# Two attention-mixer layers on one core: later blocks' queries projected inside attention, with a second guard

## The chip, the core and the metric

One of the eight cores of a Trainium2 chip runs the whole kernel. The time is the device's, from start to end of one execution, in microseconds (us). The engines that matter are PE (TensorE, matmuls), ScalarE (ACT in the rows: exponentials, casts), VectorE (DVE), GpSimd (POOL) and SP (SyncE), whose queue issues nearly all DMAs.

## The reference, cut to what matters

```python
def _A_ref(x, wq, wk, wv, wo):            # x: (1, 2048, 512), 32 heads of 16
    q = (x @ wq).reshape(B, S, H, Dh).transpose(0, 2, 1, 3)
    k = x @ wk                            # one key head and one value head for all
    v = x @ wv
    scores = einsum("bhqd,bkd->bhqk", q, k) * Dh ** -0.5
    o = einsum("bhqk,bkd->bhqd", softmax(scores), v)
    return o.transpose(0, 2, 1, 3).reshape(B, S, H * Dh) @ wo

def _B_ref(x, w1, b1, w2, b2):            # MLP over the tokens, F = 1792
    u = gelu(einsum("bsd,sf->bdf", layernorm(x), w1) + b1)
    return (einsum("bdf,fs->bds", u, w2) + b2).transpose(0, 2, 1)

for layer in range(2):
    x = x + _A_ref(layernorm(x), wq, wk, wv, wo)
    x = x + _B_ref(layernorm(x), w1, b1, w2, b2)
```

## The kernel before, in words

The residual x stays in SBUF as 16 tiles of 128 tokens. Four tiles make a block of 512 (NB = 4). Every layer has three parts: a projection, attention, and the MLP over the tokens, and each overlaps its neighbours where the order of the code lets it. That order is written out by hand: the order of calls is the order on every engine, and each engine takes its own instructions in it.

**Projection (class Proj).** A fp32 product is made of three products of parts: an operand is cast to a short form (hi) and the rest of it is a second tile (lo). `weights` does this for wq and wk, wv (L190 to L200; the lo parts on VectorE). For a block, `norm` and `turn` make the transposed normalized rows; `keys` (L274) gives keys and values, `key_terms` (L285) puts the keys' hi and lo parts with six DMAs (L293) into `kst`, the score's left operand; `queries(b, m)` (L315) multiplies a quarter of the query columns, which are 12 matmuls of 512 columns (L265), takes their squares on ScalarE (L323), splits them into hi (ScalarE, L271) and lo (VectorE, L272) in a tile `q2`, and puts that tile into a DRAM buffer `qd` with two DMAs of 256 KB on SP (L336), here called a pair of puts. Four quarters make a block, so sixteen products and sixteen pairs make the queries of a layer. `q2` and the key tile `ks` come from one ring of buffers with the tag "q2": three in layer 0, two in layer 1. A new tile waits until the DMAs of the one whose buffer it takes have landed.

**The shift and the guard.** Softmax is computed without a maximum: a bound made of the norms of queries (`bound`, L341: four small matmuls with `sel`) and of keys (`key_bound`, L357) is put into one extra row of both score operands and so subtracted inside the score. In before, the keys' part is written into row 0 of `kst` (L371) and copied by a DMA into row 64 (L372). Where the bound is too far off, true maxima are needed: `flag` works out whether, and `guard` (L408) reads the flag on every engine (L410) and branches (L414). For these inputs the branch is not taken. So that the wait is covered, before scores ten tiles ahead of the guard (`Attention.ahead`, L621) and splits a query product in two around other work (`within`, L266).

**Attention (class Attention).** A group is four heads of one block of queries; 8 groups to a block, 32 in a layer. `load_group` (L471) brings a group's operands from `qd` into one of two tiles `qs` by four DMAs. A group has 32 tiles of scores, each of 2x512 columns: two matmuls (L581), one exponential of 128x1024 on ScalarE (L588), two matmuls that sum into one PSUM bank (L594); VectorE evicts the bank at a group's end (L504). `run` (L652) interleaves tiles and other PE work in turns: LONG holds 12 tiles and one fill, SHORT 8 tiles and a fill, PLAIN 2 tiles without. Fills of the class Mixer are products of w1 (L795, from group 8 on) and output projections (L570, from group 4 on).

**MLP.** After attention, `second` (L965) multiplies with w2, bound by PE. Layer 1's projection is woven into layer 0's `second` stage for blocks 0 to 2, and the rest of it comes as a tail behind that stage.

```python
LONG = (3, 0, 3, -4, 2, -2, 2, -2, 2, -4)
SHORT = (2, 0, 2, -4, 2, -2, 2, -2)
PLAIN = (2, -2)
```

A positive number scores so many tiles, a negative one sums so many, 0 is the fill.

Of the kernel before, what the change touches and what calls it, by code (L numbers as in the profile page):

```python
# [8 lines left out]
F32 = mybir.dt.float32  # L9
# [9 lines left out]
P = 128  # L19
S, D, H, DH, F = 2048, 512, 32, 16, 1792  # L20
NB = 4
# [16 lines left out]
AHEAD = 2  # L38
# [7 lines left out]
def kernel(  # L46
# [43 lines left out]
    k2m = cp.tile([1, NB], F32, tag="k2m", name="k2m")  # L90
    qd = dp.tile([NB * NG, R1, 4, 2, QB], F32, tag="qd", name="qd")
# [9 lines left out]
    def constants():  # L101
# [15 lines left out]
        for i in range(NQ):  # L117
            for r in (0, HALF):
                nc.gpsimd.memset(f32(qs[i][r : r + 1]), 1.0)
# [15 lines left out]
    def stats(ts_, name):  # L135
        n = len(ts_)
        st = sm.tile([P, 4, 6], F32, tag="st", name=f"st_{name}")
        mv = sm.tile([P, 4, 2], F32, tag="mv", name=f"mv_{name}")
        for i, t in enumerate(ts_):
            nc.vector.bn_stats(st[:, i, :], x[t])  # L140
        for i, t in enumerate(ts_):
            nc.vector.bn_aggr(mv[:, i, :], st[:, i, :])
        return mv[:, :n, :]

    def rstd(mv, twice, name):
        n = mv.shape[1]
        w = sm.tile([P, 4, 4], F32, tag="rw", name=f"rw_{name}")
# [26 lines left out]
    class Proj:  # L174
        def __init__(self, layer):
            self.l = layer
            self.sides = 0
            self.sq, self.h, self.hT, self.kv, self.kk = {}, {}, {}, {}, {}
            self.pool = pool(f"proj{layer}")
            p = self.pool  # L180
            self.wq = p.tile([P, ND, 2, D], F32R, tag="wq", name=f"wq{layer}")
            self.wkv = p.tile([P, ND, 2, 2 * DH], F32R, tag="wkv", name=f"wkv{layer}")
            self.c2 = p.tile([H, 2, QB], F32R, tag="c2", name=f"c2_{layer}")

        def weights(self):
            p, n = self.pool, self.l
            nc.gpsimd.memset(f32(self.c2), 0.0)
            for kt in range(ND):
                raw = p.tile([P, D], F32, tag="tmp", bufs=7 - 3 * n, name=f"wqr{n}_{kt}")
                nc.sync.dma_start(raw, wq_d[kt * P : (kt + 1) * P, :])  # L190
                nc.scalar.copy(self.wq[:, kt, 0, :], raw)
                nc.vector.tensor_tensor(
                    self.wq[:, kt, 1, :], raw, f32(self.wq[:, kt, 0, :]), op=ALU.subtract
                )
            raw = p.tile([P, ND, 2 * DH], F32, tag="kvr", name=f"wkvr{n}")
            nc.sync.dma_start(raw[:, :, :DH], wk_d.rearrange("(t p) c -> p t c", p=P))
            nc.sync.dma_start(raw[:, :, DH:], wv_d.rearrange("(t p) c -> p t c", p=P))
            nc.vector.tensor_copy(self.wkv[:, :, 0, :], raw)
            nc.vector.tensor_tensor(
                self.wkv[:, :, 1, :], raw, f32(self.wkv[:, :, 0, :]), op=ALU.subtract  # L200
            )

        def stats(self, ts_):
            self.mv = stats(ts_, f"a{self.l}_{ts_[0]}")

        def scales(self, ts_):
            n, mv, k = self.l, self.mv, len(ts_)
            y = rstd(mv, False, f"a{n}_{ts_[0]}")
            my = sm.tile([P, 4], F32, tag="my", name=f"my{n}_{ts_[0]}")
# [3 lines left out]
            self.y = y, my  # L213

        def norm(self, ts_, scalar=True):
            p, n = self.pool, self.l
            y, my = self.y
            for i, t in enumerate(ts_):
                self.h[t] = p.tile([P, D], F32, tag="tmp", bufs=7 - 3 * n, name=f"h{n}_{t}")
# [4 lines left out]
                else:  # L224
                    normed(self.h[t], t, self.mv, y, i)

        def turn(self, ts_):

            p, n, k = self.pool, self.l, len(ts_)
            b, c = ts_[0] // 4, ts_[0] % 4 * P  # L230
            if c == 0 and b not in self.hT:
                self.hT[b] = p.tile([P, ND, 2, QB], F32R, tag="hT", bufs=2 - n, name=f"hT{n}_{b}")
# [26 lines left out]
        def product(self, out, w, cols, b, within=None):  # L259
            k, hT = 0, self.hT[b]  # L260
            for kt in range(ND):
# [5 lines left out]
                if within and kt == 1:  # L267
                    within()

# [862 lines left out]
```

## Time and profile before

| what | us |
|---|---|
| median of 3 runs | 2712.18 |
| lowest and highest run | 2710.46, 2713.71 |
| the profiled execution | 2709.55 |
| its span (first to last instruction) | 2707.8 |
| PE busy | 2637.9 (97%) |
| ScalarE busy | 2126.4 (79%) |
| exponentials (2048 of 128x1024) | 1907.1, 1.057 each |
| VectorE busy | 818.4 (30%) |
| GpSimd busy | 87.3 (3%) |

The profile is of one execution; its rows give a start time, a length, the engine, the line (L), the operation with the names of output and input, shapes and a count, and in brackets how long the engine stood idle just before and what released it. SPq is the queue of SP. A busy PE is not the same as PE at its peak: when the exponentials set the pace, its matmuls are stretched.

### The profile page before, as it was taken

To read this page: it belongs to the slowest core of one execution; us is meant where nothing else is said; L and a number is where in the kernel's file an instruction comes from. 1 tells how busy PE (TensorE), PEld (TensorE's weight loads), DVE (VectorE), ACT (ScalarE), POOL (GpSimd) and SP (SyncE) were. 2 spreads that over 40 slices of the span, in tenths; PEclk is the share of its full clock that TensorE was granted. 3 is DMA by queue.
4 is the path that set the end of the run, shared out by engine and by line. 5 is a ranking of instruction groups with operands and counts; after the bars stand their busy time and mean duration, and the time that the engine had idled before them with its cause. 6 is when DMAs were issued, how large, how long until landed. Compare 5 with 4: busy or idle time off the path is not lost. (4 is left out here: it accounts for less than half of the span.)

```text
span 2707.8 us, 40615 instructions
## 1 busy us (share of the span) xinstructions
PE 2637.9 (97%) x16062; PEld 1225.8 (45%) x16062; DVE 818.4 (30%) x1835; ACT 2126.4 (79%) x2399; POOL 87.3 (3%) x124
## 2 busy tenths in 40 slices
PE   7699999999999999999998999999999999999999
PEld 4323333433444343368774333344434333434787
DVE  6312123223322332155443111322242224222532
ACT  3389999899898999953325999998898999997511
POOL 1000000000000000040000000000000000001300
PEclk9899999999999999999999999999999999999999
DMA  3210011111111011023332101011111111110343
GB/s 129 94 49 21 23 35 38 45 30 34 38 38 35 26 42 31 11 78 113 107 102 73 30 21 35 23 44 30 41 28 39 38 41 32 38 25 14 110 123 99
DMA packets 159553, 135.51 MB, mean 50 GB/s; under 512 B 12862, under 2 KB 127612, under 8 KB 159356
## 3 DMA queue, kind: packets, MB, share of 16 engines
q1 hardware_dynamic: 159356, 132.85, 16.9%
q8 instruction: 128, 2.10, 0.3%
q14 instruction: 69, 0.57, 0.1%
HBM read 93.47 MB, written 22.02 MB: 43 GB/s over the span
## 5 line engine op out<-in xcount | busy, mean ns | idle before, releaser
L588 ACT ACTIVATE p<-sc 128x1024 f32<-128x1024 f32 x2048 | 1907.1, 1057 | 161.4 <-PE sc L581 161.4
L594 PE MATMUL acc<-p,vaug 128*32 128x512 f32 x8192 | 1124.0, 603 | 0.3 <-DVE q L272 0.3
L581 PE MATMUL sc<-qs,kst 51*128 51x512 f32 x4096 | 737.5, 442 | 28.2 <-DMA kst<-kst 8.9
L581 PEld LDWEIGHTS sc<-qs,kst 51*128 51x128 f32 x4096 | 318.8, 185 | 777.9 <-issue 514.5
L594 PEld LDWEIGHTS acc<-p,vaug 128*32 128x32 f32 x8192 | 233.0, 108 | 442.4 <-issue 412.3
L965 PE MATMUL py<-u,w 128*128 128x512 f32 x1344 | 307.7, 390 | 0.0
L965 PEld LDWEIGHTS py<-u,w 128*128 128x128 f32 x1344 | 251.8, 188 | 53.1 <-issue 0.7
L795 PE MATMUL pu<-hb,w 128*128 128x512 f32 x984 | 248.4, 401 | 0.4 <-POOL w L782 0.4
L795 PEld LDWEIGHTS pu<-hb,w 128*128 128x128 f32 x984 | 178.4, 188 | 59.8 <-issue 15.2
L953 ACT CAST w<-w2r 128x896 fp32r<-128x896 f32 x64 | 60.0, 944 | 181.7 <-PE py L965 164.0
L504 DVE COPY ev<-acc 128x512 f32<-128x512 f32 x64 | 44.3, 692 | 518.8 <-PE acc L594 518.4
L524 DVE RECIPROCAL o<-o 128x128 f32<-128x128 f32 x120 | 113.6, 947 | 99.8 <-DMA o<-ev 99.8
L573 DVE TENSOR_TENSOR x<-x,po 128x512 f32<-128x512 f32 x64 | 44.0, 688 | 311.5 <-PE po L570 311.5
L803 DVE TENSOR_TENSOR ua<-ua,pu 128x512 f32<-128x512 f32 x54 | 36.9, 687 | 324.6 <-PE pu L795 324.6
L782 POOL TENSOR_TENSOR w<-w1r,w 128x256 fp32r<-128x256 f32 x74 | 59.1, 816 | 2214.7 <-ACT w L780 2214.7
L265 PE MATMUL pq<-hT,wq 128*128 128x512 f32 x384 | 101.5, 417 | 0.1
L570 PE MATMUL po<-wo,hl 128*128 128x512 f32 x360 | 100.4, 412 | 0.9 <-DVE ev L504 0.6
L954 DVE TENSOR_TENSOR w<-w2r,w 128x896 fp32r<-128x896 f32 x64 | 69.8, 1091 | 101.7 <-ACT w L953 101.0
L795 PE MATMUL pu_l<-hb,w 128*128 128x512 f32 x336 | 80.1, 394 | 4.9 <-POOL hb L895 3.4
L265 PEld LDWEIGHTS pq<-hT,wq 128*128 128x128 f32 x384 | 75.0, 200 | 21.0 <-issue 3.0
L801 DVE COPY ua<-pu 128x512 f32<-128x512 f32 x28 | 19.4, 692 | 199.0 <-PE pu L795 199.0
L570 PEld LDWEIGHTS po<-wo,hl 128*128 128x128 f32 x360 | 62.6, 188 | 35.0 <-issue 19.3
(129 smaller groups left out, 913.2 us busy)
## 6 DMA issues: line engine op xcount, KB each, us to landing
w1r<-in_B_w_dram SPq DMA_DIRECT2D x224, 128.0 KB
w2r<-in_B_w_dram SPq DMA_DIRECT2D x64, 448.0 KB
qs<-qd SPq DMA_DIRECT2D x128, 136.0 KB
qd<-q SPq DMA_DIRECT2D x64, 256.0 KB
o<-ev SPq DMA_DIRECT2D x120, 128.0 KB
qs<-qd SPq DMA_DIRECT2D x128, 64.0 KB
x<-in_A_x_dram SPq DMA_DIRECT2D x16, 256.0 KB
out_dram<-x SPq DMA_DIRECT2D x16, 256.0 KB
```

What stands on the lines that cost most here:

```text
L265: nc.tensor.matmul(out, a, c, start=(k == 0), stop=(k == 3 * ND - 1))
L504: nc.vector.tensor_copy(ev, acc)
L524: nc.vector.reciprocal(o[:, 1, c], o[:, 1, c])
L570: nc.tensor.matmul(po, a, c, start=(k == 0), stop=(k == 3 * len(parts) - 1))
L581: nc.tensor.matmul(sc[:, j, :], kst[rows, kt * P : (kt + 1) * P], qs[i % NQ][rows, j0 // 2, :], start=True, stop=True,)
L588: nc.scalar.activation(pt, sc, AF.Exp, scale=0.25)
L594: nc.tensor.matmul(self.acc[i][c : c + 32, :], vaug[:, kt].rearrange("p d k -> p (d k)"), pt[:, j, :], start=(kt == 0), stop=(kt == NKT - ...
L782: eng.tensor_tensor(w[:, 1], raw, f32(w[:, 0]), op=ALU.subtract)
L795: nc.tensor.matmul(pu, a, c, start=(start and k == 0), stop=(stop and k == 5))
L953: nc.scalar.copy(w[:, 0], raw)
L954: nc.vector.tensor_tensor(w[:, 1], raw, f32(w[:, 0]), op=ALU.subtract)
L965: nc.tensor.matmul(py, a, d, start=(c == 0 and f == 0 and k == 0), stop=(c == 1 and f == NFH - 1 and k == 2),)
```

## The change

Constant NOW = (1, 3) says how many blocks of queries are projected before attention begins: one in layer 0, three in layer 1. The other blocks' products, shifts and the minimum over their bounds come as fills of attention's first turns (`later`): in layer 0 twelve LONG and four SHORT turns, 176 tiles from the start of group 0 on; in layer 1 four LONG and two SHORT. A fill writes the spare one of the two accumulator banks; both its parts hi and lo are made on VectorE, its squares on GpSimd. A second guard for the later blocks stands between the tiles where those blocks begin, after 8 groups in layer 0 and after 24 in layer 1. The Mixer's pools open when the last of these fills is done.

The keys' part of the bound leaves the score: rows 0 and 64 of `kst` and `qs` become zero, and a small matmul with a row of ones (`onerow`) spreads a quarter of the keys' bound to 128 partitions (`kb`), which each exponential adds as its bias. No tile is scored ahead of the guard, no product is split, and no put is held back until after it.

In layer 0 the weights are issued on ScalarE's queue, so the loads of x follow one another on SP; the lo parts of weights and of keys go from VectorE to GpSimd, and GpSimd's constants now stand behind the weights' lo parts. The statistics of blocks 2 and 3 are taken together. The ring of `q2` and `ks` has two buffers in both layers, and in layer 0 keys and queries take turns in it. In layer 1, products (2, 0) and (2, 1) move from the stage of w2 into the tail behind it, and block 3's four products into attention.

```diff
-AHEAD = 2
+NOW = (1, 3)
...
         nc.gpsimd.memset(f32(kst), 1.0)
-        for i in range(NQ):
-            for r in (0, HALF):
-                nc.gpsimd.memset(f32(qs[i][r : r + 1]), 1.0)
+        nc.gpsimd.memset(onerow, 1.0)
+        for r in (0, HALF):
+            nc.gpsimd.memset(f32(kst[r : r + 1]), 0.0)
+            for i in range(NQ):
+                nc.gpsimd.memset(f32(qs[i][r : r + 1]), 0.0)
...
         def weights(self):
             p, n = self.pool, self.l
+            issue = nc.sync if n else nc.scalar
...
+            nc.scalar.copy(self.wkv[:, :, 0, :], raw)
+            nc.gpsimd.tensor_tensor(
                 self.wkv[:, :, 1, :], raw, f32(self.wkv[:, :, 0, :]), op=ALU.subtract
             )
+            for kt in range(ND):
+                nc.scalar.copy(self.wq[:, kt, 0, :], raws[kt])
+                nc.gpsimd.tensor_tensor(
+                    self.wq[:, kt, 1, :], raws[kt], f32(self.wq[:, kt, 0, :]), op=ALU.subtract
+                )
...
-            ks = p.tile([DH, 2, QB], F32R, tag="q2", bufs=3 - n, name=f"ks{n}_{b}")
-            self.split(ks, kv[:DH, :])
+            ks = self.keep.tile([DH, 2, QB], F32R, tag="q2", bufs=2, name=f"ks{n}_{b}")
+            nc.scalar.copy(ks[:, 0, :], kv[:DH, :])
+            nc.gpsimd.tensor_tensor(ks[:, 1, :], kv[:DH, :], f32(ks[:, 0, :]), op=ALU.subtract)
...
+        def queries(self, b, m, pq=None):
+            k, n = self.keep, self.l
+            during = pq is not None
+            if not during:
+                pq = bank2(f"pq{n}_{b}_{m}")[:, 0, :]
+            self.product(pq, self.wq, slice(m * P, (m + 1) * P), b)
+            q2 = k.tile([P, 2, QB], F32R, tag="q2", bufs=2, name=f"q2_{n}_{b}_{m}")
+            sq = self.sq[b, m] = k.tile([P, QB], BF16, tag="sq", bufs=5, name=f"sq{n}_{b}_{m}")
+            (nc.vector.tensor_copy if during else nc.scalar.copy)(q2[:, 0, :], pq)
+            nc.vector.tensor_tensor(q2[:, 1, :], pq, f32(q2[:, 0, :]), op=ALU.subtract)
+            if during:
+                nc.gpsimd.tensor_tensor(sq, f32(q2[:, 0, :]), f32(q2[:, 0, :]), op=ALU.mult)
             else:
+                nc.scalar.activation(sq, pq, AF.Square)
...
         def key_bound(self):
...
-            self.key_shift(k2)
-            self.k2 = k2
+            pb = self.side(f"pkb{n}")
+            nc.tensor.matmul(pb[:, :1], onerow, k2, start=True, stop=True)
+            nc.vector.tensor_scalar(kb, pb[:, :1], 0.25, None, op0=ALU.mult)
...
+        def later(self):
+            n, now = self.l, NOW[self.l]
+            work = []
+            for b in range(now, NB):
+                for m in range(ND):
+                    work.append((LONG, lambda i, b=b, m=m: self.queries(b, m, bank(i, f"pq{n}_{b}_{m}"))))
+                work.append((SHORT, lambda i, b=b: self.shifts(b, bank(i, f"pc{n}_{b}"))))
+            work.append((SHORT, lambda i: self.lowest(now, NB, bank(i, f"pg{n}_{now}"))))
+            return work
...
-            nc.scalar.activation(pt, sc, AF.Exp, scale=0.25)
+            nc.scalar.activation(pt, sc, AF.Exp, bias=kb, scale=0.25)
...
+            second_guard = 2 * NKT * NG * NOW[self.l]
+            later = proj.later()
             while self.scored < total:
                 mix.chores(self)
-                turn = mix.turn() if len(self.pend) == LAG else PLAIN
+                turn, part = PLAIN, None
+                if len(self.pend) == LAG:
+                    if later:
+                        turn, part = later[0]
+                    else:
+                        turn, part = mix.turn(), lambda i: mix.fill(self, i)
...
+                if self.scored == second_guard:
+                    proj.guard(proj.flagged, NOW[self.l], NB)
...
+    proj.shifts(0)
+    proj.key_bound()
+    proj.lowest(0, NOW[0])
+    proj.first_groups()
+    proj.first_guard()
...
             proj.scales(tiles(b)[3:])
             proj.norm(tiles(b)[3:], False)
+            proj.queries(b - 1, 0)
+            proj.turn(tiles(b)[:2])
+            proj.queries(b - 1, 1)
+            proj.turn(tiles(b)[2:])
             proj.queries(b - 1, 2)
-            proj.turn(tiles(b)[:2])
+            proj.keys(b)
             proj.queries(b - 1, 3)
-            proj.turn(tiles(b)[2:])
-            proj.keys(b)
-            proj.last_keys()
```

Where instructions stand, first on SP in layer 0's projection, behind the loads of x. In a name such as q_0_1_0 the figures are layer, block and quarter; ks_1 is block 1's keys. Before:

```order
L293 DMA kst<-ks_0_267 16x512 x6
L336 DMA qd<-q_0_0_0_289 4x16x1024 x2
L336 DMA qd<-q_0_0_1_323 4x16x1024 x2
L336 DMA qd<-q_0_0_2_355 4x16x1024 x2
L336 DMA qd<-q_0_0_3_399 4x16x1024 x2
L293 DMA kst<-ks_1_439 16x512 x6
L355 DMA qd<-c_0_110 8x4x1024
L336 DMA qd<-q_0_1_0_469 4x16x1024 x2
L336 DMA qd<-q_0_1_1_503 4x16x1024 x2
```

And in the changed kernel, at the same place:

```order
L303 DMA kst<-ks_0_329 16x512 x6
L341 DMA qd<-q_0_0_0_351 4x16x1024 x2
L303 DMA kst<-ks_1_415 16x512 x6
L341 DMA qd<-q_0_0_1_437 4x16x1024 x2
L303 DMA kst<-ks_2_507 16x512 x6
L341 DMA qd<-q_0_0_2_529 4x16x1024 x2
L303 DMA kst<-ks_3_573 16x512 x6
L341 DMA qd<-q_0_0_3_595 4x16x1024 x2
L422 DMA qd<-c_0_111 8x4x1024
```

The keys of all four blocks now stand between the four pairs of block 0's puts, and the twelve pairs of later blocks are gone from here.

Next GpSimd at the start of the changed kernel: lo parts of weights (wkv, wq), constants, and the keys' square (kk) and lo part (ks).

```order
L207 TENSOR_TENSOR wkv_115<-wkvr_151,wkv_115 128x4x32
L212 TENSOR_TENSOR wq_110<-wqr_0_152,wq_110 128x512
L212 TENSOR_TENSOR wq_110<-wqr_1_156,wq_110 128x512
L212 TENSOR_TENSOR wq_110<-wqr_2_158,wq_110 128x512
L212 TENSOR_TENSOR wq_110<-wqr_3_160,wq_110 128x512
L106 MEMSET ones 128x1
```

In before, GpSimd's row ahead of the same constants is the memset of c:

```order
L187 MEMSET c_0_110 32x1024
L104 MEMSET ones 128x1
L105 MEMSET sel 128x128
L108 AFFINE_SELECT sel<-sel 128x32
L112 AFFINE_SELECT sel<-sel 128x32
```

The five subtractions, which wait for the weights' loads, now stand ahead of all constants and of what follows them.

Last PE in layer 1's tail, behind the w2 stage; pq is a query product, pk a key product, pt the transposes, sc a score. Before:

```order
L265 MATMUL pq_2_2_12371<-hT_2_12056,wq_10941 128x512 x12
L238 MATMUL pt_12_12391<-ident,h_12_12293 128x128 x4
L238 MATMUL pt_12_12391<-ident,h_13_12295 128x128 x4
L265 MATMUL pq_2_3_12402<-hT_2_12056,wq_10941 128x512 x12
L238 MATMUL pt_14_12422<-ident,h_14_12297 128x128 x4
L238 MATMUL pt_14_12422<-ident,h_15_12369 128x128 x4
L265 MATMUL pk_3_12433<-hT_3_12348,wkv_10942 32x512 x12
```

In the changed kernel:

```order
L280 MATMUL pq_2_0_12439<-hT_2_12164,wq_11048 128x512 x12
L253 MATMUL pt_12_12459<-ident,h_12_12361 128x128 x4
L253 MATMUL pt_12_12459<-ident,h_13_12363 128x128 x4
L280 MATMUL pq_2_1_12470<-hT_2_12164,wq_11048 128x512 x12
L253 MATMUL pt_14_12490<-ident,h_14_12365 128x128 x4
L253 MATMUL pt_14_12490<-ident,h_15_12437 128x128 x4
L280 MATMUL pq_2_2_12501<-hT_2_12164,wq_11048 128x512 x12
L280 MATMUL pk_3_12521<-hT_3_12416,wkv_11053 32x512 x12
L280 MATMUL pq_2_3_12538<-hT_2_12164,wq_11048 128x512 x12
```

Block 2's four products stand in the tail, where two stood, and behind them, in place of block 3's products and ten tiles of scores, come only the small steps of the bound and the guard.

More of the change, by code (lines that the diff above doesn't have):

```diff
@@ L187, in weights @@
             nc.gpsimd.memset(f32(self.c2), 0.0)
+            raw = p.tile([P, ND, 2 * DH], F32, tag="kvr", name=f"wkvr{n}")
+            raws = []
             for kt in range(ND):
[L189 to L194, printed above, removed]
@@ L696, in __init__, with open @@
             self.tail = False
+        def open(self):
+            n = self.l
+            self.ap = pool(f"uacc{n}")
+            self.wp = pool(f"w1p{n}")
+            self.hp = pool(f"hp{n}")
+            self.uacc = [self.ap.tile([P, D], F32, tag=f"ua{f}", name=f"ua{n}_{f}") for f in range(NF)]
         def warm(self, func):
```

379 lines of the change are left out of this document (158 added, 221 removed).

## The prediction

> **What bounds the kernel now.** I read the table of stretches first, then the evictions that end each attention group, then the waits of the first 145 us, and last the rows around the puts of the queries. The first table gives, per stretch, its length and each engine's busy time, with the granted TensorE clock, the DMA share and GB/s.
>
> ```profile
> core 0 of [0], span 2707.8 us
> 0.00:50.00 50.00, 32.84 (x141) 22.44 (x141) 32.97 (x90) 17.41 (x26) 11.14 (x25) 1.00 0.43 144
> 50.00:100.00 50.00, 40.59 (x173) 27.29 (x173) 22.95 (x50) 20.97 (x33) 1.03 (x1) 0.93 0.30 95
> 100.00:120.00 20.00, 2.82 (x6) 1.62 (x7) 2.55 (x4) 2.46 (x4) 0.00 (x0) 0.60 0.28 101
> 200.00:300.00 100.00, 100.00 (x654) 33.82 (x656) 18.41 (x39) 96.85 (x106) 0.00 (x0) 1.00 0.07 22
> ```
>
> Between 200 and 300 us ScalarE is busy for 96.85 of 100 us: plain attention is bound by its exponentials. Before that no engine is: PE stands idle for 17.2 us of the first fifty and 9.4 of the next, and from 100 to 120 almost everything does. The start is a chain of waits:
>
> ```profile
> ACT q L271 <- DMA qd<-q: 20.8, 8, 3.9
> ACT ks L271 <- DMA qd<-q: 11.6, 3, 4.4
> PE sc L581 <- SPq L414: 5.4, 1, 5.4
> ```
>
> In 20 to 145 us ScalarE's split of a query or key tile waits 32.4 us (20.8 + 11.6) for an earlier tile's put to land, because all pass through one small ring of buffers; the guard then holds the first score 5.4 us more. How long a put takes, and where attention starts:
>
> ```profile
> 56.90 0.60 SPq L336 DMA_DIRECT2D qd<-q  x1
> 67.06 0.59 ACT L271 CAST q<-pq 128x512 fp32r<-128x512 f32 x1 [3.65 <-DMA qd<-q]
> 92.36 0.59 ACT L271 CAST q<-pq 128x512 fp32r<-128x512 f32 x1 [3.62 <-DMA qd<-q]
> 97.34 0.59 ACT L271 CAST q<-pq 128x512 fp32r<-128x512 f32 x1 [0.44 <-DMA qd<-q]
> 102.32 0.59 ACT L271 CAST q<-pq 128x512 fp32r<-128x512 f32 x1 [2.38 <-DMA qd<-q]
> 128.82 0.61 SPq L336 DMA_DIRECT2D qd<-q  x1
> 140.11 0.76 PE L581 MATMUL sc<-qs,kst 51*128 51x512 f32 x1 [5.39 <-SPq L414]
> 165.14 0.69 DVE L504 COPY ev<-acc 128x512 f32<-128x512 f32 x1 [6.57 <-PE acc L594]
> 194.48 0.69 DVE L504 COPY ev<-acc 128x512 f32<-128x512 f32 x1 [28.64 <-PE acc L594]
> 1492.42 0.69 DVE L504 COPY ev<-acc 128x512 f32<-128x512 f32 x1 [4.31 <-PE acc L594]
> 1521.75 0.69 DVE L504 COPY ev<-acc 128x512 f32<-128x512 f32 x1 [28.64 <-PE acc L594]
> ```
>
> A pair of puts that starts at 56.90 frees its buffer at 67.06, 10.2 us later; with several pairs queued one lands every 5.0 us (92.36, 97.34, 102.32). A group takes 29.33 us in both layers (194.48 - 165.14, 1521.75 - 1492.42). I take about 1.3 us from a group's last exponential to its eviction, an estimate from the 1.06 us of its last sums (row at 1467.57 below) and a wait. So attention runs as if it had begun undisturbed at 165.14 - 29.33 - 1.3 = 134.5 us in layer 0 and at 1492.42 - 29.33 - 1.3 = 1461.8 us in layer 1. These two starts are what the change moves; what it adds inside attention is set against them.
>
> **Layer 0, the start.** Only block 0's queries go ahead of attention: four products and four pairs of puts instead of sixteen. The ring now has two buffers, and keys and queries take turns in it, so query tile m waits for the landing of tile m-1's pair. The lo parts of weights and keys move to GpSimd, ahead of its constants.
>
> ```profile
> 8.95 0.62 ACT L191 CAST wq<-wqr 128x512 fp32r<-128x512 f32 x1
> 16.67 0.62 ACT L191 CAST wq<-wqr 128x512 fp32r<-128x512 f32 x1 [7.10 <-DMA wqr<-in_A_wq_dram]
> L895 POOL TENSOR_TENSOR hb<-ht,hb 128x512 fp32r<-128x512 f32 x4 | 5.1, 1269 | 9.5 <-ACT hb L893 9.5
> L119 POOL MEMSET qs<- 1x1024 f32 x4 | 3.8, 943 | 0.1
> L282 POOL TENSOR_TENSOR kk<-kv 16x512 bf16<-16x512 f32 x6 | 6.2, 1030 | 228.7 <-ACT kv L279 228.7
> L116 POOL MEMSET kst<- 128x2048 f32 x1 | 1.8, 1804 | 0.0
> 27.23 3.79 SPq L293 DMA_DIRECT2D kst<-ks  x6
> ```
>
> GpSimd starts on the weights at some 14 us (between the casts at 8.95 and 16.67) and needs 4 x 1.27 + 0.3 = 5.4. The constants follow: 1.8 for kst, 3.8 for the four rows of qs, the same again for two new rows of 2048 in kst, some 2 for small ones, 11.4 in all: 31. Then the keys' square and their lo part, 1.03 each: 33. Four of the six kst DMAs wait for that lo part, 4 x 0.63 = 2.5, and block 0's first pair is issued at 35.5 (bounds 31, where the old order had it, and 42, where GpSimd starts late). Then each turn is a landing of 10.2, the cast 0.59, the lo part (0.69, VectorE's time for this shape in the evictions above), and by estimate 0.4 for handing over: 11.9. The fourth pair is issued at 35.5 + 3 x 11.9 = 71.2 and lands at 81.4. PE has a query product and a key product in such a turn, 3.0 each (row at 66.77 below), and transposes and small steps of some 2.4 by estimate, 8.4 in all, and stays covered. The loads of the first groups follow; the same eight in layer 1:
>
> ```profile
> 1389.93 0.72 SPq L476 DMA_DIRECT2D qs<-qd  x1
> 1394.83 1.05 SPq L477 DMA_DIRECT2D qs<-qd  x1
> 1399.12 0.97 DVE L272 TENSOR_TENSOR ks<-kv,ks 16x512 fp32r<-16x512 f32 x1 [1.98 <-DMA qs<-qd]
> ```
>
> From the first issue to landing they take 1399.1 - 1389.9 = 9.2, so that the guard's queue is clear and the first exponential runs at 81.4 + 9.2 = 90.6. If the loads wait only for the shifts' put and not for the last pair, it is 84; if the first pair is late, 97. Layer 0 starts 134.5 - 90.6 = 43.9 us earlier.
>
> **Layer 0, inside attention.** Twelve products of twelve matmuls come back as fills. What a fill costs there is shown by the w1 fills in later groups, which have the same size and the same turn of twelve tiles:
>
> ```profile
> 765.65 3.02 PE L795 MATMUL pu<-hb,w 128*128 128x512 f32 x12
> 778.07 1.20 PE L795 MATMUL pu<-hb,w 128*128 128x512 f32 x4
> 66.77 2.99 PE L265 MATMUL pq<-hT,wq 128*128 128x512 f32 x12
> 119.06 5.49 PE L265 MATMUL pq<-hT,wq 128*128 128x512 f32 x12
> 1467.57 1.06 PE L594 MATMUL acc<-p,vaug 128*32 128x512 f32 x8
> 1469.60 0.83 PE L581 MATMUL sc<-qs,kst 51*128 51x512 f32 x4 [0.96 <-ACTq L414]
> ```
>
> Twelve tiles with a fill take 778.07 - 765.65 = 12.42, without one 12 x 29.33 / 32 = 11.00: a fill costs 1.42, not its 3.02, as the exponentials cover the rest. Twelve of them: 17.0. The three shifts and the minimum are 13 small matmuls, 13 x 3.02 / 12 = 3.3 at most, of which the share of a fill shows, 1.42 of 3.02: 1.5. The casts and lo parts go to VectorE (18.4 of 100 us busy), the squares to GpSimd (idle): nothing, under that cover; the puts and their ring have 12 us per turn and land in 10.2, two turns apart: nothing, and if it were something, the fill's own lo part would wait, while ScalarE and PE go on. The keys' bound as a bias of the exponential: no row shows an exponential with one; between -0.01 and +0.01 us on each of 2048, I take nothing. The second guard stands between two groups; behind its read on SP are later group loads, on PE the next score, on ScalarE the next exponential. Its price lies between layer 1's first guard, where PE waited 0.96, and layer 0's, 5.39 (above): I take 1.0, since the last puts are then far back. The first product after a standing start is slow, 5.49 against 2.99 (the clock is 0.60 in that stretch), and no tile scored ahead hides it: 2.5. In all 17.0 + 1.5 + 1.0 + 2.5 = 22.0, and layer 0 gains 43.9 - 22.0 = 21.9.
>
> **Layer 1.** Two of block 2's products leave the stage of the second weights, where PE is the bound, for the tail; block 3's queries go into attention.
>
> ```profile
> 1410.40 3.02 PE L265 MATMUL pq<-hT,wq 128*128 128x512 f32 x12
> 1423.32 0.85 PE L265 MATMUL pq<-hT,wq 128*128 128x512 f32 x3
> ```
>
> The stage ends at 1423.3 - 2 x 3.02 = 1417.3, called t. The first pair is issued at t + 5.6 (a product, then layer 0's split and hand-over) and lands at t + 15.8, the second 5.0 behind it, t + 20.8. The third, which needs the first's buffer, is issued at t + 17.1 and lands at t + 27.3; block 3's keys need the third's buffer: cast and lo part to t + 29, six kst DMAs to t + 32.8, landed and first exponential at t + 35 = 1452.3. That is 9.5 earlier than 1461.8. Inside attention come 4 x 1.42 = 5.7 of fills, 0.6 of shifts, a guard of 1.0 and the cold start of 2.5: 9.8. Layer 1 loses 0.3. Both layers: 21.6 faster. The profiled execution took 2709.55 (span 2707.8), 2.6 below the median 2712.18 of the runs, so 2688.0 there and about 2690 as a median.
>
> **Two rules of the Trainium skill.** The first is about the put. "DMA: Bandwidth & Descriptors", section "Why a DMA increments its semaphore by 16 and not by 1", says that a transfer runs on the largest number of engines up to 16 that divides the slowest dimension on both sides, which is 4 for a put of 4x16x1024; with the page's 27 GiB/s for each engine and some 2 us fixed, an estimate for a pair is 6.5 us, by which the sum would be some 16 us lower. The trace has 10.2, and the measurement decides. The other speaks against the move to GpSimd. In the trace a tiny VectorE step beside GpSimd's memset took 0.89 us, and alone 0.17:
>
> ```profile
> 8.04 0.89 DVE L149 TENSOR_SCALAR rw_a<-mv_a 128x4 f32<-128x4 f32 x1
> 23.83 0.17 DVE L149 TENSOR_SCALAR rw_a<-mv_a 128x4 f32<-128x4 f32 x1
> ```
>
> "SBUF — State Buffer", section "Who interferes with whom", has the two engines share a pair of ports under an exclusive lock, which would explain those rows. If the seven or so VectorE steps of the prologue's chain met GpSimd like this, 7 x 0.72 = 5 us would be added to block 0's start, inside its bound of 42.
>
> **The rivals.** (a) *Lone pairs land sooner.* If the 10.2 is mostly queue, a pair alone would take 5.0 of traffic and 1.5 of way, and the turn falls to PE's 8.4: 3 x 3.5 and 3.7 on the last landing in layer 0, some 3 in layer 1, 17 in all: 2673. For it: the 5.0 between landings. Against it: the pair of 128.82 had no query put beside it, and PE went on only at 140.11. (b) *Fills cost their full 3.02*, because ScalarE's lead is only two tiles: 16 x 1.6 = 25.6 more, 2716, the same as before. Against it: the 12.42 of the w1 fills. (c) *The two-buffer ring becomes the bound and the kernel slower.* Three buffers at 5.0 us each put a pair some 15 us under way in the loaded queue. Each us of landing counts four times in layer 0 and about 2.5 times in layer 1, 6.5 in all, so it decides from 10.2 + 21.6 / 6.5 = 13.5 us; at 15 the time is 2690 + 4.8 x 6.5 = 2721. Against it: only one pair is ever under way in layer 0. (d) *The second guards cost what layer 0's first did*, 5.4 each: 2 x 4.4 more, 2699; with a first pair at 42 as well 2705, and 2708 with a cold start of 2.5 behind one. For it: the branch waits for whatever the queue still has under way.
>
> **How the numbers follow.** The forecast as it stands, 2680 to 2697, has 0.62; (a) 0.14, (b) 0.06, (c) 0.08, (d) 0.10. The range reaches from (a)'s 2672 to 2708, (d) with a late first pair, and leaves out (b), (c) and the outer part of (a). A measurement here can tell 0.2%, 5.4 us: faster is the forecast, (a) and (d), 0.86; the same is most of (b), 0.06; slower is (c) and the end of (b), 0.08.
>
> **What would show it.** The first eviction of layer 0 at about 90.6 + 1.3 + 29.33, with 2.6 fills of 1.42 in that group and the cold start, 127 us where 165.14 stands; pairs of block 0 issued 11.9 apart; the eight evictions of groups 0 to 7 with 12 x 1.42 beyond 29.33 each; layer 1's first exponential near t + 35. I am wrong if the turns are 8 or 15 us, if a fill costs 2 us or more, or if either second guard leaves PE idle for over 3 us.

## The result, and the profile after

The changed kernel takes 2823.12 us as a median of 4 runs (2821.6 to 2823.99), before takes 2711.32 in the same comparison: a ratio of 1.0411, with a 95% interval of 1.0393 to 1.0429. It is 112 us slower, where 21 us faster was forecast. The profiled execution has a span of 2822.3 us.

The first look is at the stretch in which plain attention runs. The columns are those of the prediction's table: length, then busy time of PE, PEld, VectorE, ScalarE and GpSimd, the granted clock, the DMA share, GB/s.

```profile
20.00:100.00 80.00, 44.66 (x174) 25.59 (x174) 30.59 (x63) 24.64 (x36) 21.68 (x28) 0.73 0.17 47
300.00:400.00 100.00, 99.58 (x610) 32.26 (x610) 23.02 (x52) 98.25 (x98) 0.00 (x0) 1.00 0.12 30
```

ScalarE is as full as before (98.25 of 100 us), but it gets through 98 exponentials and not through 106. The evictions of the changed kernel tell the same (start time, then length), two in layer 0 and two plain groups of layer 1:

```profile
145.10 0.69 DVE L507 COPY ev<-acc 128x512 f32<-128x512 f32 x1 [4.77 <-PE acc L597]
382.40 0.69 DVE L507 COPY ev<-acc 128x512 f32<-128x512 f32 x1 [23.44 <-PE acc L597]
1576.19 0.69 DVE L507 COPY ev<-acc 128x512 f32<-128x512 f32 x1 [6.28 <-PE acc L597]
1608.35 0.69 DVE L507 COPY ev<-acc 128x512 f32<-128x512 f32 x1 [17.76 <-PE acc L597]
```

A plain group takes 32.16 us (1608.35 - 1576.19) where it took 29.33: 2.83 us more on 32 exponentials, 0.088 each. So the lead of the early start is gone by the end of group 7 and then grows the other way:

| eviction of | before | after | difference |
|---|---|---|---|
| layer 0, group 0 | 165.14 | 145.10 | -20.0 |
| layer 0, group 7 | 374.47 | 382.40 | +7.9 |
| layer 0, group 31 | 1157.89 | 1208.67 | +50.8 |
| layer 1, group 0 | 1492.42 | 1544.19 | +51.8 |
| layer 1, group 31 | 2485.13 | 2599.20 | +114.1 |

Nothing is lost between the layers (50.8 to 51.8); all of it is lost inside attention. From group 8 of layer 0 on every group is longer than before, also those that hold neither a moved product nor a guard. The start of layer 0 in the changed kernel: the first and last pair of block 0's puts, the first load, the first score and the first exponential; and the first exponential of layer 1.

```profile
38.77 0.69 SPq L341 DMA_DIRECT2D qd<-q  x1
77.90 0.60 SPq L341 DMA_DIRECT2D qd<-q  x1
89.12 0.72 SPq L479 DMA_DIRECT2D qs<-qd  x1
104.11 1.42 PE L584 MATMUL sc<-qs,kst 51*128 51x512 f32 x4 [23.04 <-SPq L396]
105.14 1.11 ACT L591 ACTIVATE p<-sc,kb 128x1024 f32<-128x1024 f32 x1 [27.18 <-PE sc L584]
...
1503.33 1.11 ACT L591 ACTIVATE p<-sc,kb 128x1024 f32<-128x1024 f32 x1 [8.02 <-PE sc L584]
```

The start is early, but at 105.14, not at 90.6. Two questions follow: is it the bias that slows every exponential, and where did 14.5 us of the start go?

### The profile page after: what moved, and what is told of

It reads as the page before. It is cut to its first block, busy times and chain, and to the rows that moved or that the text cites. A ratio compares the mean times of both kernels' runs of the same rounds, so it can differ in the third digit from the quotient of the medians.

```text
span 2822.3 us, 40676 instructions
## 1 busy us (share of the span) xinstructions
PE 2727.0 (97%) x16070; PEld 1239.2 (44%) x16070; DVE 816.5 (29%) x1829; ACT 2283.2 (81%) x2368; POOL 130.4 (5%) x161
## 5 line engine op out<-in xcount | busy, mean ns | idle before, releaser
L591 ACT ACTIVATE p<-sc,kb 128x1024 f32<-128x1024 f32 x2048 | 2079.7, 1153 | 152.6 <-PE sc L584 151.4
L597 PE MATMUL acc<-p,vaug 128*32 128x512 f32 x8192 | 1145.8, 602 | 0.0
L584 PE MATMUL sc<-qs,kst 51*128 51x512 f32 x4096 | 793.5, 455 | 45.1 <-SPq L396 30.0
L584 PEld LDWEIGHTS sc<-qs,kst 51*128 51x128 f32 x4096 | 328.7, 185 | 842.7 <-issue 454.9
L573 PEld LDWEIGHTS po<-wo,hl 128*128 128x128 f32 x360 | 62.6, 188 | 35.1 <-issue 19.0
```

The lines of the kernel that those rows point to most:

```text
L573: nc.tensor.matmul(po, a, c, start=(k == 0), stop=(k == 3 * len(parts) - 1))
L584: nc.tensor.matmul(sc[:, j, :], kst[rows, kt * P : (kt + 1) * P], qs[i % NQ][rows, j0 // 2, :], start=True, stop=True,)
L591: nc.scalar.activation(pt, sc, AF.Exp, bias=kb, scale=0.25)
L597: nc.tensor.matmul(self.acc[i][c : c + 32, :], vaug[:, kt].rearrange("p d k -> p (d k)"), pt[:, j, :], start=(kt == 0), stop=(kt == NKT - ...
```

## Experiments on the bias

**Without the bias.** In the changed kernel, the exponentials lose their bias operand; this version leaves the keys' part of the bound out of the exponent.

```diff
-            nc.scalar.activation(pt, sc, AF.Exp, bias=kb, scale=0.25)
+            nc.scalar.activation(pt, sc, AF.Exp, scale=0.25)
```

> The changed kernel with the bias operand taken off the exponentials; the keys' part of the bound is left out of the exponent, all else stays (its matmul and its copy too). Theory A (each exponential pays about 0.09 us for a bias that it reads from a tile: plain groups 32.16 us in the changed kernel against 29.33 before): plain groups return to 29.33 and the time falls by about 131 us, which is 8 groups x 2.83 + 42.9 over groups 8 to 31 of layer 0, and 2 x 2.83 + 59.6 in layer 1: 2692, between 2685 and 2706. Theory B (the products inside attention, the guards and the ring of two buffers cost it): plain groups stay at 32 and the time at 2790 or above.

Measured: 2703.08 us, ratio to before 0.9969 (0.9956 to 0.9981). Rows of this run: the first exponential, the end of group 7, and a plain group of layer 1.

```profile
105.00 1.94 ACT L591 ACTIVATE p<-sc 128x1024 f32<-128x1024 f32 x2 [27.90 <-PE sc L584]
...
368.38 0.69 DVE L507 COPY ev<-acc 128x512 f32<-128x512 f32 x1 [20.71 <-PE acc L597]
...
1545.63 0.69 DVE L507 COPY ev<-acc 128x512 f32<-128x512 f32 x1 [15.07 <-PE acc L597]
1574.96 0.69 DVE L507 COPY ev<-acc 128x512 f32<-128x512 f32 x1 [28.64 <-PE acc L597]
```

A plain group is back at 29.33 and 120.0 us are gone (2823.12 - 2703.08). Theory B, that the moved products, the guards and the ring cost it, falls: they are all still there. The rest of the change is a gain, but of some 8 us.

**Before, with a bias of zeros.** The same operand alone, in the kernel before:

```diff
+    kb = cp.tile([P, 1], F32, tag="kb", name="kb")
+    nc.vector.memset(kb, 0.0)
...
-            nc.scalar.activation(pt, sc, AF.Exp, scale=0.25)
+            nc.scalar.activation(pt, sc, AF.Exp, bias=kb, scale=0.25)
```

> The kernel before, with a tile of 128x1 zeros, written once at the start, as the bias of the exponentials; nothing else. Theory A: plain groups 32.16, and 2711 + 131 = 2842, between 2830 and 2855. Theory B: 2711 as before. Theory C (it is not the operand but the wait for a tile that is written late, between the bound and the first score): 2711 too, as these zeros are there from the start.

Measured: 2837.67 us, ratio 1.0466 (1.045 to 1.0482), 126.4 us more than its before, 2711.27. Two evictions of layer 0:

```profile
200.02 0.69 DVE L506 COPY ev<-acc 128x512 f32<-128x512 f32 x1 [31.45 <-PE acc L596]
232.16 0.69 DVE L506 COPY ev<-acc 128x512 f32<-128x512 f32 x1 [17.75 <-PE acc L596]
```

The group takes 32.14 us with a tile that has been there since the start, so it is the operand and not a wait for it.

**Before, with bias and scale from tiles.** The edit is as in the run before it, with a second tile of 0.25:

```diff
+    ksc = cp.tile([P, 1], F32, tag="ksc", name="ksc")
+    nc.vector.memset(ksc, 0.25)
...
+            nc.scalar.activation(pt, sc, AF.Exp, bias=kb, scale=ksc)
```

> The kernel before, with both the bias (zeros) and the scale (0.25) of the exponentials read from tiles of 128x1. If every such operand has its own price, plain groups take 29.33 + 2 x 2.83 = 35.0 and, with all of attention bound by ScalarE by now, the time is 2842 + 2048 x 0.088 = 3022, between 2990 and 3030. If the price is that of reading operands from a tile at all, once, it is 2842 with groups of 32.16. Theory B: 2711.

Measured: 2968.04 us in one run. Two evictions:

```profile
201.97 0.69 DVE L508 COPY ev<-acc 128x512 f32<-128x512 f32 x1 [34.35 <-PE acc L598]
237.01 0.69 DVE L508 COPY ev<-acc 128x512 f32<-128x512 f32 x1 [21.16 <-PE acc L598]
```

The plain group takes 35.04, another 2.90 and so 0.091 us for each exponential: every operand that is read from a tile has its own price. The total came 22 us under the lower end of what was expected: the sum was made as though all groups were bound by ScalarE, while in groups 8 to 29 of layer 0, most of which hold fills, the second operand added only 0.8 to 2.5 us (group 10 goes 34.81, 36.67, 38.96). That PE still sets part of their time would explain it; no run tests that by itself.

The Trainium skill states this price: "ScalarE: Activation LUTs", section "What ACT_TABLE_LOAD costs", has each [128,1] pointer operand add some 93 ns to an activation. The 88 and 91 ns measured here agree with it.

**The bound back in the row.** All of the change but its bias: the keys' part goes to row 0 of kst and by DMA to row 64, as before.

```diff
-            pb = self.side(f"pkb{n}")
-            nc.tensor.matmul(pb[:, :1], onerow, k2, start=True, stop=True)
-            nc.vector.tensor_scalar(kb, pb[:, :1], 0.25, None, op0=ALU.mult)
+            key_shift(k2)
...
-            nc.scalar.activation(pt, sc, AF.Exp, bias=kb, scale=0.25)
+            nc.scalar.activation(pt, sc, AF.Exp, scale=0.25)
```

> The changed kernel with the keys' part of the bound put back where it was before, in row 0 of kst and by a DMA in row 64, and the rows of qs at one; no bias, no matmul for it, and the two long memsets of kst rows are gone from GpSimd. All else of the change stays. Theory A: as without the bias, and up to 3.6 us better for GpSimd's shorter start: 2686 to 2704. Theory B: 2790 or above.

Measured: 2701.29 us, ratio 0.9965 (0.9951 to 0.9979). It is faster than both kernels. In it the first pair is issued at 35.74, since two memsets of 1x2048 are gone from GpSimd, and the first exponential comes at 102.67.

## Experiments on the start of layer 0

Each of these stands on the kernel with the bound in the row, and each adds its edit to the one before it, except where it says otherwise. Their comparisons had a before of 2712.6 to 2714.0, so ratios are compared.

**GpSimd's constants first.** The calls of `weights` and `constants` change places.

> The kernel with the bound back in the row (2701.3 there), and GpSimd's constants ahead of the weights' lo parts again, as before the change. Theory A (GpSimd's order held block 0's first pair back): the first pair of puts is issued 1 to 3 us earlier than 35.74 and every turn follows: 2698 to 2700. Theory B (layer 0's start is bound by PE and the transposes between, where each key product runs at a low granted clock, 5.3 us against 2.9 in layer 1): no change, 2700 to 2702. Theory C (VectorE's small steps get slow beside GpSimd's memsets, 0.89 against 0.17 us): block 0's normalization is late by up to 5 us and so is all else: 2703 to 2706.

Measured: ratio 0.9966 (0.9953 to 0.998), the same as without the edit. By the trace it is theory C: block 0's first pair is issued at 39.28, later and not earlier than 35.74, and the first exponential comes at 104.39. VectorE's rows in this run, beside GpSimd's:

```profile
17.49 0.16 DVE L154 TENSOR_SCALAR rw_a<-rw_a 128x4 int32<-128x4 int32 x1
17.68 1.23 DVE L155 TENSOR_SCALAR rw_a<-rw_a 128x4 int32<-128x4 int32 x1
18.94 1.18 DVE L159 TENSOR_TENSOR rw_a<-rw_a 128x4 f32<-128x4 f32 x1
```

```profile
17.61 4.93 POOL L207 TENSOR_TENSOR wq<-wqr,wq 128x512 fp32r<-128x512 f32 x4
```

From 17.61 to 22.5, while GpSimd subtracts, a step of 128x4 takes as long as one of GpSimd's subtractions, 1.2 us, and alone 0.16; the memsets do the same to the steps at 8 to 11 us. That is the exclusive lock of which the prediction cited the Trainium skill, "SBUF — State Buffer", section "Who interferes with whom", and the trace agrees. By the first pair the order of the change, constants last, is the better one; the ratios do not tell the two apart.

**One group of loads ahead of the guard.**

```diff
-    proj.first_groups()
+    load_group(qs[0], 0)
     proj.first_guard()
+    load_group(qs[1], 1)
```

> As the run with the constants first, and group 1's four loads issued behind the first guard of layer 0, so that only group 0's four stand ahead of it. In the run with the bound in the row the eight are issued from 86.67 on and the first score comes 15.3 us later. Theory A (the guard waits for the loads to land, and they are served one after the other): the first score comes 6 to 7 us earlier, some 2694 on top of what the constants do. Theory B (the branch itself is the cost): only the issue of four loads goes, 2.7 us.

Measured: ratio 0.9947 (0.9932 to 0.9962). First load and first exponential in this run:

```profile
88.26 0.72 SPq L480 DMA_DIRECT2D qs<-qd  x1
98.03 1.02 ACT L592 ACTIVATE p<-sc 128x1024 f32<-128x1024 f32 x1 [21.39 <-PE sc L585]
```

From the first load to the first exponential it takes 9.8 us for four loads and took 16.3 for eight (88.06 to 104.39 in the run with the constants first): theory A, the guard waits for the loads to land, and eight take longer than four.

**The last pair held back.** Block 0's quarter 3, which groups 6 and 7 read, is put behind the first guard (and inside its branch, if that is taken).

```diff
+            if n == 0 and b == 0 and m == ND - 1:
+                self.held = b, m, q2
+            else:
+                put_queries(b, m, q2)
...
     load_group(qs[1], 1)
+    put_queries(*proj.held)
```

> As the run before it, and block 0's last pair of puts (quarter 3, which groups 6 and 7 read) issued behind the first guard, so that the shifts' put and group 0's loads do not queue behind 512 KB. Theory A (the loads wait for the shifts' put, which lands behind that pair, 77.39 to 86.67): the loads start 5 to 7 us earlier and the first score with them, some 2688. Theory B (the loads wait for something else of PE or VectorE): no more than 1 us.

Measured: ratio 0.9948 (0.9934 to 0.9962), no change, although the first exponential comes 7.2 us earlier. ScalarE's rows show where it went:

```profile
90.79 4.69 ACT L600 ACTIVATE p<-sc 128x1024 f32<-128x1024 f32 x5 [15.04 <-PE sc L593]
98.56 8.44 ACT L600 ACTIVATE p<-sc 128x1024 f32<-128x1024 f32 x9 [3.08 <-PE sc L593]
107.21 2.85 ACT L600 ACTIVATE p<-sc 128x1024 f32<-128x1024 f32 x3 [0.21 <-PE sc L593]
118.16 4.69 ACT L600 ACTIVATE p<-sc 128x1024 f32<-128x1024 f32 x5 [8.09 <-PE sc L593]
```

The theory of the loads was right, and the gain was given back at 110 to 118. The rows of VectorE and PE there, in the same run:

```profile
104.43 0.43 DVE L506 CAST wo<-wor 128x512 fp32r<-128x512 f32 x1 [24.11 <-DMA wor<-in_A_wo_dram]
...
110.77 0.68 DVE L329 CAST q<-pq 128x512 fp32r<-128x512 f32 x1
111.48 0.69 DVE L330 TENSOR_TENSOR q<-pq,q 128x512 fp32r<-128x512 f32 x1
...
112.23 5.39 PE L275 MATMUL pq<-hT,wq 128*128 128x512 f32 x12 [4.61 <-DVE q L330]
```

VectorE takes its work in the order of the code. It stands for 24.11 us at the cast of wo, and the first fill's cast comes after it; PE's second fill needs the bank that this cast reads. The loads of wo are issued behind the guard, from 93.92 on, and in this run also behind the held pair. After its wait the second fill's product takes 5.39 us, where it took 3.02 in the run before.

**Spare matmuls.** Six matmuls that nothing reads stand ahead of the key products of blocks 1 to 3.

```diff
+        def spin(self, b, count):
+            out = bank2(f"spin{b}")[:, 0, :]
+            for k in range(count):
+                nc.tensor.matmul(
+                    out, self.wq[:, 0, 0, :P], self.hT[b][:, 0, 0, :],
+                    start=(k == 0), stop=(k == count - 1),
+                )
...
+            proj.spin(b, 6)
             proj.keys(b + 1)
```

> As the run before it, and six spare matmuls of 512 columns on PE ahead of the key products of blocks 1 to 3 in layer 0, whose result nothing reads, in the time when PE waits for the transposed rows. Theory A (the short waits lower the granted clock, and the key product of 12 matmuls takes 5.3 us in place of 2.9): key products at 3 us, the turns 2 us shorter each, some 2683. Theory B (the clock has other reasons): the spare matmuls delay what follows, 0 to 4 us longer than the run before it.

Measured: ratio 0.9944 (0.9931 to 0.9958), the same as without them. The key product of block 3, first in the held-pair run, to which the matmuls were added, then with them:

```profile
65.35 0.41 PE L275 MATMUL pk<-hT,wkv 128*32 128x512 f32 x1 [2.92 <-ACT hT L253]
66.61 4.09 PE L275 MATMUL pk<-hT,wkv 128*32 128x512 f32 x11 [0.84 <-DVE hT L254]
```

```profile
63.59 0.43 PE L275 MATMUL pk<-hT,wkv 128*32 128x512 f32 x1 [0.41 <-ACT hT L253]
64.85 2.71 PE L275 MATMUL pk<-hT,wkv 128*32 128x512 f32 x11 [0.83 <-DVE hT L254]
```

With spare matmuls all three key products take 3.1 us, and the granted clock is 1.00 in each of the three stretches of 10 us from 40 to 70; the held-pair run has 0.71, 1.00 and 0.83 there. So far theory A holds: with more work on PE the product is fast. But short waits do not by themselves make it slow. This is the key product of block 2, first with the bound in the row, then in the held-pair run, which has no spare matmuls:

```profile
50.24 0.41 PE L275 MATMUL pk<-hT,wkv 128*32 128x512 f32 x1 [1.25 <-ACT hT L253]
51.50 4.90 PE L275 MATMUL pk<-hT,wkv 128*32 128x512 f32 x11 [0.84 <-DVE hT L254]
```

```profile
52.78 0.42 PE L275 MATMUL pk<-hT,wkv 128*32 128x512 f32 x1 [1.25 <-ACT hT L253]
54.04 2.71 PE L275 MATMUL pk<-hT,wkv 128*32 128x512 f32 x11 [0.84 <-DVE hT L254]
```

The same two waits stand before 5.3 us in one run and 3.1 us in the other. What makes the clock differ (0.66 and 1.00 from 50 to 60 us) stays open.

Pairs of puts are now issued at 38.87, 50.74 and 62.58, 11.9 apart. The ring sets this: ScalarE's casts wait for the landing of the pair before.

```profile
49.01 0.58 ACT L337 CAST q<-pq 128x512 fp32r<-128x512 f32 x1 [2.15 <-DMA qd<-q]
60.69 0.59 ACT L337 CAST q<-pq 128x512 fp32r<-128x512 f32 x1 [2.00 <-DMA qd<-q]
```

In the held-pair run the pairs stand at 38.80, 52.52 and 63.79, so only one turn was long there. Little could be gained: 1.2 us at the third pair, and 0.4 at the first exponential (90.37 against 90.79).

**wo on GpSimd.** On the held-pair run (no spare matmuls): the constants again behind the weights, and in layer 0 wo's casts and lo parts on GpSimd.

```diff
-                nc.vector.tensor_copy(self.wo[:, kt, 0, :], raw)
-                nc.vector.tensor_tensor(
+                eng = nc.vector if n else nc.gpsimd
+                eng.tensor_copy(self.wo[:, kt, 0, :], raw)
+                eng.tensor_tensor(
```

> As the run with the held pair, but with GpSimd's constants behind the weights' lo parts as the change has them, and in layer 0 the cast and the lo part of wo on GpSimd in place of VectorE. In the held-pair run the first exponential came at 90.79, as early as the prediction had it, but ScalarE then waited 8.09 us at 118: the first fill's cast stood on VectorE behind wo's casts, which waited for wo's loads, and PE's second fill needs that bank. Theory A (that is where the gain went): the wait is gone, the first exponential comes some 2 us earlier for the order of the constants, and the time is 8 to 10 us below the held-pair run: a ratio to before of 0.991, some 2687. Theory B (the second fill waits for the held pair to land anyway): the wait moves to the ring and the ratio stays at 0.994 to 0.995.

Measured: 2691.61 us, ratio 0.9918 (0.9904 to 0.9931). ScalarE at the same place:

```profile
89.35 4.69 ACT L601 ACTIVATE p<-sc 128x1024 f32<-128x1024 f32 x5 [14.93 <-PE sc L594]
97.86 8.44 ACT L601 ACTIVATE p<-sc 128x1024 f32<-128x1024 f32 x9 [3.82 <-PE sc L594]
106.51 2.86 ACT L601 ACTIVATE p<-sc 128x1024 f32<-128x1024 f32 x3 [0.21 <-PE sc L594]
110.39 8.36 ACT L601 ACTIVATE p<-sc 128x1024 f32<-128x1024 f32 x9 [1.02 <-PE sc L594]
```

The wait of 8.09 is 1.02, theory A. Of the two changes in this edit, the order of the constants can account for the first exponential, 1.4 us earlier than in the held-pair run; the first eviction comes 7.7 us earlier (136.18 to 128.47), and the rest goes with the wait that has shrunk. With spare matmuls added to this kernel:

> As the run with wo on GpSimd, with the six spare matmuls ahead of each key product. With them the key products took 3.1 to 3.4 us and pairs of puts were issued 11.9 us apart (38.87, 50.74, 62.58), which is the ring of two alone; so the granted clock and the ring cost nearly the same. Expected by that: no more than 1.5 us better than without them. If the clock were the bound: 4 to 6 us better.

Measured: 2690.82 us, ratio 0.9915 (0.9902 to 0.9929): within what was expected, and not to be told from the run without them.

**Loads of 16 partitions.** On the run with wo on GpSimd, the shape of a group's loads:

```diff
-            nc.sync.dma_start(f32(dst[r : r + 2 * R1]), src[e])
-            nc.sync.dma_start(f32(dst[r + 2 * R1 : r + 2 * R1 + DH]), src[e, 0, :DH])
+            for t, s in ((r, 0), (r + R1, 1), (r + 2 * R1, 0)):
+                nc.sync.dma_start(f32(dst[t : t + DH]), src[e, s, :DH])
+            for s in range(2):
+                t = r + s * R1 + DH
+                nc.sync.dma_start(f32(dst[t : t + 1]), src[e, s, DH : DH + 1])
```

> As the run with wo on GpSimd, but a group's loads cut differently: six of 16 partitions and four of one partition (the shifts' rows) in place of two of 34 and two of 16 partitions; the same bytes. While the loads of 34 partitions are under way the trace shows a flat 50 GB/s, as two of the 16 DMA engines would give. Theory A (34 partitions are served by two engines): from the issue of the last load ahead of the guard to the first score it takes 3 us or less in place of 6.6, which is eaten by six more issues of 0.65 us: first exponential at 88.5 to 90 (89.35 without the cut), the time the same within 2 us. Theory B (a fixed delay of the loads or of the branch): the 6.6 us stay, the first exponential comes at 93 and the time is 3 to 4 us longer.

Measured: ratio 0.9923 (0.9907 to 0.994), the same time. The DMA traffic from 78 to 92 us in slices of 0.35 us, first with loads of 34 partitions (the run with wo on GpSimd), then with loads of 16:

```profile
DMA  4001000113117530001111111100000001011434
GB/s 187 0 0 24 0 0 6 53 47 94 53 53 135 193 123 12 29 23 76 53 47 53 53 53 47 53 12 0 0 0 0 0 0 23 29 53 53 76 99 152
```

```profile
DMA  0032536001013233200000000000221343001022
GB/s 18 0 105 88 117 117 182 23 0 23 0 41 123 105 100 105 88 12 23 0 12 0 0 0 0 23 0 0 100 88 41 146 76 111 12 0 12 0 94 94
```

The flat stretch of some 53 GB/s that ends the loads of 34 is gone, and from the end of the last issue (82.63 + 1.69) to the first score (86.43) it takes 2.1 us in place of 6.6. As expected, six more issues eat it: from the first load to the first exponential it takes 10.1 us and took 10.6. The first exponential itself comes at 87.46, ahead of the 88.5 to 90 expected, mostly because the loads begin 1.5 us earlier in this execution. The Trainium skill has a rule that fits, "DMA: Bandwidth & Descriptors", section "Why a DMA increments its semaphore by 16 and not by 1": the engines used must divide the slowest dimension on both sides, which for 34 partitions is two, and for 16 is 16. The edit changes the other side too, from two parts (hi and lo) as the slowest dimension in `qd` to 16 rows, and by the rule that alone would give two engines as well; no run tells the two sides apart. Two engines at the page's 27 GiB/s would make 58 GB/s, an estimate; the trace has 53.

## Why the prediction was wrong, point by point

**The bias.** The step that failed is "no row shows an exponential with one; between -0.01 and +0.01 us on each of 2048, I take nothing". It was 0.088 us on each, 120.0 us in the changed kernel and 126.4 in before, and it is the whole of the sign. It is less than 2048 x 0.088 = 180, since in groups with fills less of it shows (with a bias of zeros group 10 of layer 0 grew by 1.86 us, a plain group by 2.81). No rival held this term either; the slowest of them came to 2721. The range of plus and minus 0.01 had no row behind it, and rows were there. These are groups of before, of one shape in SBUF: one with a bias from a tile (b1c), a plain cast, and one with bias and scale from tiles.

```profile
L934 ACT ACTIVATE ua<-ua,b1c 128x512 f32<-128x512 f32 x28 | 20.3, 724 | 14.4 <-DVE ua L803 14.1
L221 ACT ACTIVATE h<-x,my,rw_a 128x512 f32<-128x512 f32 x27 | 19.8, 806 | 24.6 <-DVE my L210 24.6
L935 ACT CAST u<-ua 128x512 fp32r<-128x512 f32 x28 | 17.4, 622 | 0.9
```

The means are 622, 724 and 806 ns: about 0.1 us for every operand from a tile, another function notwithstanding. That step should have read "between 0 and 0.1 on each of 2048, up to 200 us", the largest term of the sum, and the forecast would have been slower.

**The start of layer 0.** "Layer 0 starts 134.5 - 90.6 = 43.9 us earlier" was 134.5 - 105.1 = 29.4. The last pair was issued at 77.90 and not at 71.2: the first pair was 3.3 late (GpSimd began on the weights at 17.0, not at 14, and all behind it followed), and two turns came out at 13.7 and 13.6, with key products of 5.3 to 5.5 us where the prediction had 3.0. The loads began 11.2 after that pair, not 10.2. And from the first load to the first exponential it took 16.0, not 9.2; that is the largest miss, 6.8. The row at 1399.12 was read there as the landing of the eighth load. But VectorE's step needs ScalarE's cast of the same tile, and starts as that cast ends, at 1399.09 in this row of before:

```profile
1398.47 0.62 ACT L271 CAST ks<-kv 16x512 fp32r<-16x512 f32 x1
```

So 9.2 timed the cast and no landing. The runs with four loads and with loads of 16 partitions show two parts of the 16.0: the second group's loads and the shape of the loads.

**Inside attention of layer 0** the sum said 22.0. Without the bias, it is (368.38 - 105.00) - (374.47 - 134.5) = 23.4, and the same at the end of group 31: the sum held, and rival (b), with 1.6 more for each fill, is out.

**The second guards**, at 1.0 each, cost less. PE waits 0.41 at the first of them in the changed kernel, and without the bias group 23 of layer 1, at whose end the other stands, takes 0.74 us more than in before (31.67 against 30.93). So rival (d) is out.

```profile
380.51 0.59 PE L584 MATMUL sc<-qs,kst 51*128 51x512 f32 x2 [0.41 <-PEq L396]
```

**Layer 1** was right, step by step: in the changed kernel the tail begins at 1468.24, with the end of the w2 stage (t). The first pair is issued at 1473.79, 5.6 behind t as forecast; the casts that wait for the first two pairs run at 1483.82 and 1488.80, 15.6 and 20.6 behind it (15.8 and 20.8 forecast); and the first exponential comes at 1503.33, 35.1 behind it.

```profile
1468.24 2.89 PE L280 MATMUL pq<-hT,wq 128*128 128x512 f32 x12
```

Without the bias the groups up to the fourth of layer 1 end 0.6 later against layer 0's end than in before, and the last group 1.7 later, where 0.3 was forecast.

**The ring.** Rivals (a) and (c) both rested on the landing of a pair. With spare matmuls the turn is 11.9, as forecast, and a lone pair frees its buffer after 10.1 and 10.0 us (38.87 to 49.01, 50.74 to 60.69), so the 10.2 holds and neither came about. The case was slower, but not by rival (c), and its chance of 0.08 had nothing to do with what happened.

The version without the bias and with three corrections of the start ends at 2690 to 2692, near the 2690 of the forecast. That is luck and not the forecast kernel: its start needed a held pair, one group of loads less and wo on another engine to come where the sum had put it.

What stays open: in the profiled execution with wo on GpSimd, the stretch from layer 0's last eviction to layer 1's first is 337.2 us, and 334.5 in the held-pair run, at the same order of work. The run with spare matmuls, which differs from the held-pair run in layer 0's start alone, also has 337.2. So it may be a difference between executions (the runs of the held-pair kernel lie between 2697.1 and 2701.9); nothing was tried on that. What sets TensorE's clock in layer 0's start stays open too.

## What to carry to other kernels

An operand that is added to the instruction which bounds the kernel is priced first, times its count, from any row of that engine with and without such an operand, whatever its function: 0.09 us on 2048 exponentials outweighed all the rest of the change by over ten to one. In a row of the matmul's operands the same constant cost nothing here: a plain group is 29.33 us with it and without it. When a start is shortened, follow what the earlier start waits for next (here a weight's cast on an engine that works in order, which took back 6 of the 7.2 us that the held pair had won).

## What the runs showed of the hardware that was not expected

- Bias and scale read from tiles of 128x1 cost ScalarE 0.088 and 0.091 us per instruction; where it sets the pace, the distance from one exponential to the next grows by all of it.
- The loads of 34 partitions ended in a flat stretch of some 53 GB/s; with loads of 16 partitions the traffic is at 88 to 123 GB/s in most of the slices at work, and the flat stretch is gone. A pair of puts of 4x16x1024 every 5.0 us is 512 KB at 105 GB/s.
- Six spare matmuls ahead of each key product of 12 brought those of blocks 1 and 3 from 5.2 and 4.5 us to 3.1. Waits of PE of 1.25 and 0.84 us ahead of it went with 5.3 us in one run (granted clock 0.66 from 50 to 60 us) and with 3.1 in another (1.00).
- A VectorE step of 0.16 us took as long as the GpSimd instruction beside it, 1.2 us, four times in a row.
